# One PSUM buffer of two banks for the side work of the second state pass

## The chip, the cores and the metric

The kernel runs on one core of a Trainium2 chip. The metric is device time in microseconds (us) from launch to end. The median of three runs of the kernel before is 1549.19 us.

## What is computed

The reference works in three steps on x (8 batches, 8 heads, 512 tokens, 64 dimensions) and on a state of 32 rows per batch and head.

```python
scores = scale * x @ state.T          # each token reads the 32 states
xread  = softmax(scores) @ state
sread  = softmax(scale * state @ x.T) @ x   # each state reads the 512 tokens
x = concat([xread, sread])            # 8 * 544 rows of 512
x = (sigmoid(x @ w_gate) * (x @ w_val)) @ w_out      # 512 -> 1536 -> 512
out = relu(x @ w_in) ** 2 @ w_out2                   # 512 -> 2048 -> 512
```

Products are made from two fp32r parts of each operand (a high part and the rest), three matmuls for one product.

## The kernel before, in words

**Rewriting.** The rows xread are never multiplied by the gate and value weights. As xread is softmax times state, the kernel multiplies the state by the weights first (state_weights, L466) and the 512 softmax rows of a batch by the small result (front_x, L550). The gate and value weights come in 6 chunks `ch` of 256 columns, each in 4 row pieces `c` (a pair of heads), so a pass over them is 24 pieces. The states of batches 0 to 3 are the first half (m = 0), those of batches 4 to 7 the second (m = 1). There are two passes over the weights, one for each half. The change concerns the second.

**A piece of the second pass.** chunk_steps (L496) lists the steps of a chunk: load 256 KB of gate and of value weights (L118), convert them into a high and a low part (`w`, L149 on ScalarE and L150 on VectorE), then state_weights and store_g. state_weights (L466) takes two PSUM tiles `ps[0]` and `ps[1]`, called ps_g in the profile, and issues six matmuls at L474, for i in three products and in each for j in two halves: half j uses rows 64j to 64j+63 of the state and the weights and writes `ps[j]`. For i = 0 and 2 the weights' high part is read, for i = 1 the low part. Then ScalarE copies `ps[0]` (L478) and, when m is 1, VectorE copies `ps[1]` (L480) into `go`. store_g (L485) writes `go` to a DRAM tile gd; load_g (L529) reads it back as `gi`, and split_gw (L535) makes `gg` of it, the operand of front_x.

**PSUM.** The eight banks are divided among three pools: `acc` has four, `mm` two, and `at` two buffers of one bank. Every piece of work beside the units takes its tiles from `at`: state_weights (ps_g), the transposes of the states (ps_st, L231), of x (ps_xt, L306, batches 0 to 2 alone), the scores (a3, L322, ps_s2, shown as ps_s in the profile), the transposes of the other softmax (b5, L379, ps_e), the state reads (b6, L404, ps_sr) and their transposes (b7, L426, ps_so).

**Order.** The main stream of the gated layer is 108 units `(b, f)`: front (gate and value matmuls psg and psv, sigmoid, product, split) and back1 (the output matmuls into acc). Units 0 to 47 serve batches 0 to 3 and 48 to 95 batches 4 to 7; the last twelve serve the state rows. A unit calls step() six times, and step() runs what is due in `queue`, which spread() fills: a list of functions evenly over a stretch given in units. In units 25 to 55 run the six chunks of the second pass, five units for each. The scores work att_a of batch 4 is spread over units 33 to 40, of 5 over 40 to 47, of 6 over 47 to 54, of 7 over 54 to 61. The state reads att_b of batch 0 are spread over units 48 to 53.4, and each further batch starts five units later; by unit 96, split_states (L569) needs all of them. The results of the second pass are needed from unit 48 (chunk 0) to unit 58 (chunk 5, batch 4).

This list is the order of the source. The order in which each engine runs its instructions is settled when the program is built, by the framework's scheduler (`schedule_with_timeline_sim=True` in the launch): it moves an instruction ahead of others whose operands or buffers it doesn't expect to be ready. On the chip, each engine keeps to that order.

Of the kernel before, what the change touches and what calls it, by code (L numbers as in the profile page):

```python
# [8 lines left out]
F32 = mybir.dt.float32  # L9
# [6 lines left out]
PSUM = bass.MemoryType.PSUM  # L16
DRAM = bass.MemoryType.DRAM

P = 128
# [14 lines left out]
def kernel(  # L34
# [22 lines left out]
    B, H, S, D = x.shape  # L57
# [26 lines left out]
    dram = ctx.enter_context(tc.tile_pool(name="dram", bufs=1, space=DRAM))  # L84
    acc_p = ctx.enter_context(tc.tile_pool(name="acc", bufs=1, space=PSUM))
    mm_p = ctx.enter_context(tc.tile_pool(name="mm", bufs=2, space=PSUM))
    at_p = ctx.enter_context(tc.tile_pool(name="at", bufs=2, space=PSUM))


    one = ctx.enter_context(ExitStack())  # L90
# [20 lines left out]
    def load_raw(src):  # L111
        raw = raw_p.tile([P, 512, 2], U32, tag="raw", name="raw")
        flat = raw.rearrange("p a b -> p (a b)")
        for cols, ap in src:
            to = flat[:, cols]
            if len(ap.shape) == 3:
                to = to.rearrange("p (k f) -> p k f", k=ap.shape[1])
            nc.sync.dma_start(out=to, in_=ap)  # L118
        return raw
# [34 lines left out]
    def row_src(w, f):  # L154
        return [(every, w.bitcast(U32)[f * P : (f + 1) * P, :])]
# [35 lines left out]
    def mm3(ps, lh, ll, rh, rl, start, stop):  # L191
        nc.tensor.matmul(ps, lh, rh, start=start, stop=False)  # L192
        nc.tensor.matmul(ps, lh, rl, start=False, stop=False)  # L193
        nc.tensor.matmul(ps, ll, rh, start=False, stop=stop)  # L194
# [33 lines left out]
        return raw  # L228

    def prep_states(m, raw):  # L230
        ps = at_p.tile([P, 512], F32, tag="at", name="ps_st")  # L231
        for c in range(NPAIR):
            cs = slice(c * P, (c + 1) * P)
            nc.tensor.transpose(ps[:, cs], raw[:, cs], ident)
        h, l = (st_t[:, i, m].rearrange("p c n -> p (c n)") for i in range(2))
        nc.scalar.copy(out=h, in_=ps)
        nc.vector.tensor_sub(out=l, in0=ps, in1=h.bitcast(F32))
# [51 lines left out]
    def group_stages(b, g):  # L289
# [13 lines left out]
        def a2(p):  # L303
            def run():
                if by_pe:
                    xf = at_p.tile([P, S], F32, tag="at", name="ps_xt")  # L306
                    for t in range(NT):
                        ts = slice(t * P, (t + 1) * P)
                        nc.tensor.transpose(xf[:, ts], loaded_x[b, g][:, p, t, :], ident)
                else:  # L310
                    xf = f_p.tile([P, S], F32, tag="xf", name="xf", bufs=1)
                    nc.vector.transpose(xf, loaded_x[b, g][:, p, :])
                h = xx_p.tile([P, S], F32R, tag="xth", name="xth")
                l = xx_p.tile([P, S], F32R, tag="xtl", name="xtl")
                nc.scalar.copy(out=h, in_=xf)
                nc.vector.tensor_sub(out=l, in0=xf, in1=h.bitcast(F32))
                v["xt", p] = (h, l)

            return run

        def a3():
            ps = at_p.tile([P, 512], F32, tag="at", name="ps_s2")  # L322
            for p in range(2):
                h, l = v.pop(("xt", p))
                d = diag[:, :, 2 * g + p, :]
                mm3(ps, d[:, 0], d[:, 1], h, l, p == 0, p == 1)
            s2 = f_p.tile([P, S], F32, tag="s2", name="s2", bufs=1)
            nc.scalar.copy(out=s2, in_=ps)
            v["s2"] = s2
# [46 lines left out]

        def b5():
            e2 = v.pop("e2")
            ps = at_p.tile([P, 512], F32, tag="at", name="ps_e2")  # L379
            for t in range(NT):  # L380
                ts = slice(t * P, (t + 1) * P)
                nc.tensor.transpose(ps[:, ts], e2[:, ts], ident)
            et = f_p.tile([P, NT, 2, 2, 64], F32R, tag="et", name="et", bufs=1)
            pv = ps.rearrange("p (t c n) -> p t c n", t=NT, c=2)
            nc.scalar.copy(out=et[:, :, :, 0, :], in_=pv)
            nc.vector.tensor_sub(
                out=et[:, :, :, 1, :], in0=pv, in1=et[:, :, :, 0, :].bitcast(F32)
            )
            v["et"] = et
# [11 lines left out]
        def b6(p):  # L401
            def run():
                et, xs = v["et"], v.pop(("xs", p))
                ps = at_p.tile([P, 512], F32, tag="at", name="ps_sr")  # L404
                pv = ps[:, : 4 * D]
                for t in range(NT):
                    nc.tensor.matmul(
                        pv,
                        et[:, t, p].rearrange("p l n -> p (l n)"),
                        xs[:, :, :, t, :],  # L410
                        start=(t == 0),
                        stop=(t == NT - 1),
                    )
                tmp = f_p.tile([64, 2, P], F32, tag="tmp", name="tmp", bufs=1)
                if p == 0:
                    v["w"] = f_p.tile([64, 2, P], F32, tag="sw", name="sw", bufs=1)
                sv = pv.rearrange("p (l m) -> p l m", l=2)
                nc.scalar.copy(out=tmp, in_=sv[64:128])
                nc.vector.tensor_add(out=tmp, in0=sv[:64], in1=tmp)
                nc.vector.tensor_add(out=v["w"][:, p], in0=tmp[:, 0, :], in1=tmp[:, 1, :])  # L420

            return run

        def b7():
            w = v.pop("w")
            ps = at_p.tile([P, 2, 64], F32, tag="at", name="ps_so")  # L426
            for p in range(2):
                nc.tensor.transpose(ps[:, p, :], w[:, p, :], ident[:64, :64])
            for p in range(2):
                for i in range(2):  # L430
                    to = xs_t[D * p : D * (p + 1), 2 * g + i, b * NS : (b + 1) * NS]
                    src = ps[D * i : D * (i + 1), p, NS * i : NS * (i + 1)]
                    if i:
                        nc.scalar.copy(out=to, in_=src)
                    else:
                        nc.vector.tensor_copy(to, src)
# [29 lines left out]
    def state_weights(ch, c, m):  # L466
        w = gv.pop((ch, c))
        if m:
            nc.sync.dma_start(out=w_dram[ch, c], in_=w.bitcast(F32))
        ps = [at_p.tile([P, 512], F32, tag="at", name="ps_g") for j in range(2)]  # L470
        for i, (l, r) in enumerate(((0, 0), (0, 1), (1, 0))):
            for j in range(2):
                rows = slice(D * j, D * (j + 1))
                nc.tensor.matmul(  # L474
                    ps[j], st_t[rows, l, m, c, :], w[rows, r, :], start=(i == 0), stop=(i == 2)
                )
        o = go_p.tile([P, 2, 512], F32, tag="go", name="go")
        nc.scalar.copy(out=o[:, 0, :], in_=ps[0])  # L478
        if m:
            nc.vector.tensor_copy(o[:, 1, :], ps[1])  # L480
        else:
            nc.scalar.copy(out=o[:, 1, :], in_=ps[1])
        g_out[ch, c, m] = o
# [12 lines left out]
    def chunk_steps(ch, m, outs):  # L496

        raws = {}  # L500
        jobs = [("p", c) for c in range(NPAIR)] + [("o", f) for f in outs]
        steps = []

        def load(n):
            k, i = jobs[n]
            raws[n] = load_raw(pair_src(ch, i) if k == "p" else row_src(w_out1, i))

        def conv(n):
            k, i = jobs[n]
            if k == "p":  # L510
                conv_gv(ch, i, raws.pop(n))
            else:
                conv_out1(i, raws.pop(n))

        steps += [lambda: load(0), lambda: load(1)]
        for n in range(len(jobs) + 2):
            if n < len(jobs):
                steps.append(lambda n=n: conv(n))
                if n + 2 < len(jobs):
                    steps.append(lambda n=n: load(n + 2))  # L520
            if 1 <= n <= NPAIR:
                steps.append(lambda n=n: state_weights(ch, n - 1, m))
            if 2 <= n <= NPAIR + 1:
                steps.append(lambda n=n: store_g(ch, n - 2, m))
        return steps
# [244 lines left out]
    def spread(fns, start, end):  # L770

        for i, fn in enumerate(fns):
            queue.append((STEPS * (start + (end - start) * i / max(len(fns), 1)), len(queue), fn))
# [39 lines left out]
    second = []  # L813
    spread([lambda: second.append(load_states(1))], 21.5, 21.5)
    spread([lambda: prep_states(1, second.pop())], 23.5, 23.5)
    for ch in range(NCH):
        spread(chunk_steps(ch, 1, []), 25 + 5 * ch, 30 + 5 * ch)
    for b in range(QB, B):
        start = 33 + 7 * (b - QB)
        spread(att_a[b], start, start + 7)  # L820
# [96 lines left out]
```

## Time and profile before

| | |
|---|---|
| median of 3 runs | 1549.19 us (1548.54 to 1552.41) |
| the profiled execution | 1554.75 us, span 1553.0 us |
| mean granted TensorE clock | 0.980 |
| TensorE (PE) busy | 1502.7 us, 97% of the span |
| VectorE (DVE) busy | 856.6 us, 55% |
| ScalarE (ACT) busy | 724.5 us, 47% |
| second pass, first to last ps_g matmul | 246.7 to 492.9 us |

Times are us from the start of the span. PE stands for matmuls, PEld for their weight loads, SP for the DMA queue. Matmuls of a stream overlap: a row's own length (some 0.39 us) is longer than the distance from one start to the next (0.23 us), so costs on PE are taken from starts. The releaser that a row names is what ended the idle time of its engine.

### The profile page before, as it was taken

The numbers are of one execution on the slowest core, as the hardware profiler recorded it, in microseconds if no ns is written. First come the engines' busy times: TensorE is split into PE (matmuls) and PEld (weight loads), VectorE is DVE, ScalarE is ACT, GpSimd is POOL, SyncE is SP. The second block draws the span as 40 slices with busy tenths as digits, with TensorE's granted clock in tenths as the row PEclk, the third lists the DMA queues.
The fourth block names the chain that finished last, engine by engine and source line by source line (L and its number), as shares of the span: only waits on it lengthen the run. The fifth ranks groups of instructions, "written<-read, shape, count | busy, mean of one in ns | idle before, by whom it ended". The sixth has DMA issues, their size and how long they took to land.

```text
span 1553.0 us, 19161 instructions
## 1 busy us (share of the span) xinstructions
PE 1502.7 (97%) x6760; PEld 1198.6 (77%) x6760; DVE 856.6 (55%) x1550; ACT 724.5 (47%) x1314; POOL 215.2 (14%) x263
## 2 busy tenths in 40 slices
PE   5889999999998999999999999999999999999998
PEld 3568766777776778888898788888888888888887
DVE  7986896778986655555649832323232323323232
ACT  5676765456676877665435522223232222223222
POOL 1123223212332343343000000000000000000000
PEclk9789999999998999999999999999999999999999
DMA  9783788879976433342925300101010000101000
GB/s 275 232 223 96 214 275 266 275 241 256 283 209 163 147 89 111 82 122 70 392 94 159 121 27 1 55 0 54 1 55 0 28 28 0 55 0 41 1 28 15
DMA packets 173106, 185.82 MB, mean 120 GB/s; under 512 B 99537, under 2 KB 108753, under 8 KB 171985
## 3 DMA queue, kind: packets, MB, share of 16 engines
q1 hardware_dynamic: 170928, 184.07, 38.9%
q8 instruction: 53, 0.87, 0.2%
q10 hardware_dynamic: 2080, 0.52, 0.2%
q14 instruction: 45, 0.36, 0.1%
HBM read 120.59 MB, written 63.96 MB: 119 GB/s over the span
## 4 chain that ended last, share of the span: by engine, by line
PE 86%; DVE 5%; DMA 4%; ACT 2%; issue 1%; SPq 1%; POOL 0%; DVEq 0%; ACTq 0%
PE acc L193 13%; PE acc L192 13%; PE acc L194 13%; PE psi L194 8%; PE psi L192 8%; PE psi L193 8%; PE psv L192 3%; PE psg L192 3%; PE ps_g L474 3%; PE psv L193 3%; PE psv L194 3%; PE psg L193 3%; PE psg L194 3%; DMA raw<-in_moe_w_val_dram 2%; DMA gd<-go 1%
## 5 line engine op out<-in xcount | busy, mean ns | idle before, releaser
L200 DVE TENSOR_TENSOR gl<-g,gh 128x512 fp32r<-128x512 f32 (+1 forms) x252 | 181.1, 719 | 233.6 <-ACT gh L199 220.9
L199 ACT CAST gh<-g 128x512 fp32r<-128x512 f32 (+1 forms) x252 | 150.3, 596 | 241.8 <-PE acc L193 212.6
L725 DVE TENSOR_TENSOR g<-r 128x512 f32<-128x512 f32 (+1 forms) x144 | 95.4, 662 | 233.9 <-ACT r L724 233.8
L192 PE MATMUL psi<-xh,wi 128*128 128x512 f32 (+1 forms) x576 | 217.7, 378 | 2.1 <-ACT wi L149 2.1
L194 PE MATMUL psi<-xh,wi 128*128 128x512 f32 (+1 forms) x576 | 217.3, 377 | 0.2 <-DVE wi L150 0.2
L193 PE MATMUL psi<-xl,wi 128*128 128x512 f32 (+1 forms) x576 | 217.3, 377 | 0.0
L541 POOL TENSOR_TENSOR gg<-gi,gg 128x256 fp32r<-128x256 f32 x192 | 157.6, 840 | 399.6 <-ACT gg L540 392.1
L192 PE MATMUL acc<-wu,gh 128*128 128x512 f32 x544 | 212.1, 390 | 0.8 <-ACT gh L199 0.8
L193 PE MATMUL acc<-wu,gh 128*128 128x512 f32 x544 | 211.9, 389 | 0.0
L724 ACT ACTIVATE r<-psi 128x512 f32<-128x512 f32 (+1 forms) x144 | 82.7, 574 | 275.0 <-PE psi L194 275.0
L194 PE MATMUL acc<-wu,gl 128*128 128x512 f32 x544 | 206.3, 389 | 0.0
L193 PE MATMUL acc<-gl,o 128*128 128x512 f32 (+1 forms) x432 | 164.9, 383 | 1.9 <-DVE gl L200 1.8
L194 PE MATMUL acc<-gh,o 128*128 128x512 f32 (+1 forms) x432 | 163.1, 379 | 0.0
L192 PE MATMUL acc<-gh,o 128*128 128x512 f32 (+1 forms) x432 | 143.2, 386 | 0.7 <-ACT gh L199 0.7
L192 PEld LDWEIGHTS psi<-xh,wi 128*128 128x128 f32 x576 | 108.3, 188 | 24.1 <-ACT wi L149 3.8
L194 PEld LDWEIGHTS psi<-xh,wi 128*128 128x128 f32 x576 | 108.5, 188 | 20.7 <-DVE wi L150 0.7
L193 PEld LDWEIGHTS psi<-xl,wi 128*128 128x128 f32 x576 | 108.3, 188 | 20.4
L192 PEld LDWEIGHTS acc<-wu,gh 128*128 128x128 f32 x544 | 102.2, 188 | 22.5 <-ACT gh L199 1.7
L194 PEld LDWEIGHTS acc<-wu,gl 128*128 128x128 f32 x544 | 102.0, 188 | 21.3
L193 PEld LDWEIGHTS acc<-wu,gh 128*128 128x128 f32 x544 | 102.3, 188 | 20.5
L193 PEld LDWEIGHTS acc<-gl,o 128*128 128x128 f32 x432 | 81.3, 188 | 21.8 <-DVE gl L200 3.5
L192 PEld LDWEIGHTS acc<-gh,o 128*128 128x128 f32 x432 | 80.5, 190 | 20.3 <-issue 2.4
(122 smaller groups left out, 2433.1 us busy)
## 6 DMA issues: line engine op xcount, KB each, us to landing
gd<-go SPq DMA_DIRECT2D x192, 128.0 KB, 3.5
gi<-gd SPq DMA_DIRECT2D x96, 256.0 KB, 3.7
raw<-in_moe_w_out_dram SPq DMA_DIRECT2D x28, 512.0 KB, 4.6
raw<-in_moe_w_gate_dram SPq DMA_DIRECT2D x48, 256.0 KB, 4.4
raw<-in_moe_w_val_dram SPq DMA_DIRECT2D x48, 256.0 KB, 4.5
wd<-w SPq DMA_DIRECT2D x24, 512.0 KB, 4.3
ws<-wd SPq DMA_DIRECT2D x24, 512.0 KB, 8.7
xn<-in_x_dram SPq DMA_DIRECT2D x32, 256.0 KB, 3.7
```

The lines of the kernel that those rows point to most:

```text
L192: nc.tensor.matmul(ps, lh, rh, start=start, stop=False)
L193: nc.tensor.matmul(ps, lh, rl, start=False, stop=False)
L194: nc.tensor.matmul(ps, ll, rh, start=False, stop=stop)
L199: nc.scalar.copy(out=gh[:, :n], in_=g32[:, :n])
L200: nc.vector.tensor_sub(out=gl[:, :n], in0=g32[:, :n], in1=gh[:, :n].bitcast(F32))
L474: nc.tensor.matmul(ps[j], st_t[rows, l, m, c, :], w[rows, r, :], start=(i == 0), stop=(i == 2))
L541: nc.gpsimd.tensor_sub(out=t[:, 1, g], in0=src, in1=t[:, 0, g].bitcast(F32))
L724: nc.scalar.activation(out=r[:, :n], in_=ps[:, :n], func=AF.Relu)
L725: nc.vector.tensor_mul(out=g32[:, :n], in0=r[:, :n], in1=r[:, :n])
```

## The change

The pool `at` becomes a pool that is closed and opened again. From unit 24.5 to 25 on (open_at(True)) it has one buffer of two banks; from unit 55.1 on (open_at(False)) it has two buffers of one bank again. While it has the one, state_weights takes a single tile of two banks, and `ps[0]` and `ps[1]` are its halves; every other user (at_tile) takes such a tile too and uses its first bank. The matmuls, copies and DMAs are the same in kind and number, and so is the source order. In six more places (a2, a3, b5, b6, b7, prep_states) only the allocation is replaced by at_tile.

```diff
--- before.py
+++ after.py
@@ -84,7 +84,28 @@
     dram = ctx.enter_context(tc.tile_pool(name="dram", bufs=1, space=DRAM))
     acc_p = ctx.enter_context(tc.tile_pool(name="acc", bufs=1, space=PSUM))
     mm_p = ctx.enter_context(tc.tile_pool(name="mm", bufs=2, space=PSUM))
-    at_p = ctx.enter_context(tc.tile_pool(name="at", bufs=2, space=PSUM))
+
+    at = {}
+
+    def open_at(both):
+        if at:
+            at["pool"].close()
+        at["pool"], at["both"] = ExitStack(), both
+        at["tiles"] = at["pool"].enter_context(
+            tc.tile_pool(name="at", bufs=1 if both else 2, space=PSUM, reuse_waits="tile")
+        )
+
+    open_at(False)
+    ctx.callback(lambda: at["pool"].close())
+
+    def at_tile(name, shape=(P, 512)):
+        if at["both"]:
+            flat = at["tiles"].tile([P, 2, 512], F32, tag="at", name=name)[:, 0, :]
+        else:
+            flat = at["tiles"].tile([P, 512], F32, tag="at", name=name)
+        if len(shape) == 3:
+            flat = flat[:, : shape[1] * shape[2]].rearrange("p (a b) -> p a b", a=shape[1])
+        return flat
 
 
     one = ctx.enter_context(ExitStack())
@@ -228,7 +249,7 @@
         return raw
 
     def prep_states(m, raw):
-        ps = at_p.tile([P, 512], F32, tag="at", name="ps_st")
+        ps = at_tile("ps_st")
         for c in range(NPAIR):
             cs = slice(c * P, (c + 1) * P)
             nc.tensor.transpose(ps[:, cs], raw[:, cs], ident)
...
@@ -467,7 +488,11 @@
         w = gv.pop((ch, c))
         if m:
             nc.sync.dma_start(out=w_dram[ch, c], in_=w.bitcast(F32))
-        ps = [at_p.tile([P, 512], F32, tag="at", name="ps_g") for j in range(2)]
+        if at["both"]:
+            both = at["tiles"].tile([P, 2, 512], F32, tag="at", name="ps_g")
+            ps = [both[:, j, :] for j in range(2)]
+        else:
+            ps = [at_tile("ps_g") for j in range(2)]
         for i, (l, r) in enumerate(((0, 0), (0, 1), (1, 0))):
             for j in range(2):
                 rows = slice(D * j, D * (j + 1))
@@ -813,8 +838,10 @@
     second = []
     spread([lambda: second.append(load_states(1))], 21.5, 21.5)
     spread([lambda: prep_states(1, second.pop())], 23.5, 23.5)
+    spread([lambda: open_at(True)], 24.5, 25)
     for ch in range(NCH):
         spread(chunk_steps(ch, 1, []), 25 + 5 * ch, 30 + 5 * ch)
+    spread([lambda: open_at(False)], 55.1, 56)
     for b in range(QB, B):
         start = 33 + 7 * (b - QB)
         spread(att_a[b], start, start + 7)
```

## Rows read from the trace of the kernel before

**Rows 1.** The page: busy us, share of the span, instructions.

```profile
PE 1502.7 (97%) x6760; PEld 1198.6 (77%) x6760; DVE 856.6 (55%) x1550; ACT 724.5 (47%) x1314; POOL 215.2 (14%) x263
```

**Rows 2.** Stretches: us, busy by engine (instructions), granted clock, DMA share, GB/s.

```profile
300.00:400.00 100.00, 100.00 (x405) 71.44 (x404) 81.82 (x140) 59.88 (x106) 25.21 (x32) 1.00 0.86 267
400.00:430.00 30.00, 30.00 (x122) 20.99 (x121) 26.66 (x49) 19.56 (x34) 8.65 (x12) 1.00 0.90 256
...
490.00:500.00 10.00, 5.91 (x24) 4.07 (x22) 3.66 (x8) 3.88 (x7) 1.26 (x1) 0.74 0.76 203
500.00:510.00 10.00, 9.85 (x36) 7.76 (x37) 5.95 (x11) 8.49 (x18) 6.01 (x7) 0.75 0.46 106
```

**Rows 3.** The chain that ended last, from 246 to 494 us, by line.

```profile
by line: PE ps_g L474 15.7%; PE acc L193 13.3%; PE acc L192 13.1%; PE acc L194 12.8%; PE psg L192 7.3%; PE psv L192 7.3%; PE psg L194 6.5%; PE psg L193 6.4%; PE psv L193 6.2%; PE psv L194 6.1%; DMA gd<-go 1.2%; PE ps_s L193 1.2%; PE ps_s L1
```

**Rows 4.** Tile ps_g, 246 to 494 us: duration ns min/median/max, first and last start.

```profile
L474 PE MATMUL ps_g<-w,st_t x144: 386/394/502, 246.7 to 492.5; 64*128 64x512 f32 x144
```

**Rows 5.** PE's timeline: start us, us, what; a piece whose six matmuls stand together.

```profile
275.28 0.39 PE L194 MATMUL psg<-a,gg 128*128 128x512 f32 x1
275.60 0.97 PE L474 MATMUL ps_g<-w,st_t 64*128 64x512 f32 x6
...
276.82 0.39 PE L193 MATMUL psg<-a,gg 128*128 128x512 f32 x1
```

**Rows 6.** PE's timeline: halves of pieces, three matmuls at a time.

```profile
338.18 0.39 PE L192 MATMUL psg<-a,gg 128*128 128x512 f32 x1
338.50 0.96 PE L474 MATMUL ps_g<-w,st_t 64*128 64x512 f32 x3
...
339.73 0.39 PE L194 MATMUL psg<-a,gg 128*128 128x512 f32 x1
...
342.12 0.96 PE L474 MATMUL ps_g<-w,st_t 64*128 64x512 f32 x3
```

**Rows 7.** PE's timeline: four matmuls (two of each half), and two (one of each).

```profile
263.07 0.39 PE L194 MATMUL psg<-a,gg 128*128 128x512 f32 x1
263.39 0.74 PE L474 MATMUL ps_g<-w,st_t 64*128 64x512 f32 x4
...
264.40 0.40 PE L193 MATMUL psv<-a,gg 128*128 128x512 f32 x1
...
368.45 0.40 PE L194 MATMUL acc<-gh,o 128*128 128x512 f32 x1
368.77 0.50 PE L474 MATMUL ps_g<-w,st_t 64*128 64x512 f32 x2
...
369.55 0.40 PE L193 MATMUL psg<-a,gg 128*128 128x512 f32 x1
```

**Rows 8.** PE's timeline: first and last use of `at` in the crowded stretch, three holders.

```profile
316.37 0.39 PE L192 MATMUL ps_s<-xth,diag 128*128 128x512 f32 x1
...
430.85 0.60 PE L382 MATMUL ps_e<-ident,e 128*128 128x128 f32 x4
...
450.30 0.27 PE L428 MATMUL ps_so<-ident,sw 64*128 64x64 f32 x1
...
491.92 0.96 PE L474 MATMUL ps_g<-w,st_t 64*128 64x512 f32 x3
```

**Rows 9.** ScalarE's timeline: the copies that end two of these holds.

```profile
323.37 0.59 ACT L328 COPY s<-ps_s 128x512 f32<-128x512 f32 x1 [1.53 <-PE ps_s L194]
...
457.94 0.18 ACT L434 COPY xs_t<-ps_so 64x32 f32<-64x32 f32 x1
```

**Rows 10.** PE's timeline: idle time before an instruction and its releaser, 494 to 745 us.

```profile
494.87 1.22 PE L407 MATMUL ps_sr<-xs,et 128*128 128x256 f32 x4 [1.40 <-DVE et L386]
498.41 1.22 PE L407 MATMUL ps_sr<-xs,et 128*128 128x256 f32 x4 [2.32 <-POOL xs L396]
500.15 0.79 PE L192 MATMUL psg<-a,gg 128*128 128x512 f32 x1 [0.52 <-ACT gg L540]
...
744.64 0.39 PE L192 MATMUL psg<-sp,ws 128*128 128x256 f32 x1 [1.06 <-ACT sp L571]
```

More of the change, by code (lines that the diff above doesn't have):

```diff
@@ L305, in run @@
                 if by_pe:
-                    xf = at_p.tile([P, S], F32, tag="at", name="ps_xt")
+                    xf = at_tile("ps_xt")
                     for t in range(NT):
@@ L321, in a3 @@
         def a3():
-            ps = at_p.tile([P, 512], F32, tag="at", name="ps_s2")
+            ps = at_tile("ps_s2")
             for p in range(2):
@@ L378, in b5 @@
             e2 = v.pop("e2")
-            ps = at_p.tile([P, 512], F32, tag="at", name="ps_e2")
+            ps = at_tile("ps_e2")
             for t in range(NT):
@@ L403, in run @@
                 et, xs = v["et"], v.pop(("xs", p))
-                ps = at_p.tile([P, 512], F32, tag="at", name="ps_sr")
+                ps = at_tile("ps_sr")
                 pv = ps[:, : 4 * D]
@@ L425, in b7 @@
             w = v.pop("w")
-            ps = at_p.tile([P, 2, 64], F32, tag="at", name="ps_so")
+            ps = at_tile("ps_so", (P, 2, 64))
             for p in range(2):
```

## Prediction

> **What bounds the kernel.** I read the page first: PE is busy for 97% of the span, no other engine above 55% [rows 1]. That is a mean, so I asked for the stretch in which the second pass runs, some 246 to 494 us. From 300 to 430 us PE has no idle time at the full clock, VectorE is busy for 82 and then 89% and the DMA engines for 86 and 90% [rows 2]. The stage is bound by PE, with VectorE and the transfers 10 to 18% behind. Then the chain that ended last: its largest entry there, 15.7%, is the state_weights matmul of L474 [rows 3], ahead of any line of the main units, though it has only 144 matmuls there, six for each of 24 pieces [rows 4]. They cost more than their number. The timeline of PE says why, and I followed it through.
>
> A piece whose six matmuls stand together starts them in pairs: half 0 and half 1 use different rows of the array and run side by side. From the matmul before it to the second one behind it is 276.82 - 275.28 = 1.54 us [rows 5]. Two steps of the plain stream are 2 x 0.23 = 0.46 (0.455), so the visit costs **1.09 us**. Where three matmuls of one half stand alone, the same distance is 339.73 - 338.18 = 1.55, so also 1.09, for half the work; the next three stand 342.12 - 338.50 = 3.6 us later at the same price [rows 6]. Two pairs cost 264.40 - 263.07 - 0.455 = 0.87, one pair 369.55 - 368.45 - 0.455 = 0.65 [rows 7]. The price of a visit goes by how many starts follow one another, and a pair is one start.
>
> Counting all visits from 246.7 to 491.9 us in that timeline, I find 50 for the 24 pieces: 33 at about 1.08, seven at 0.86, nine at 0.63 and one at 1.31, together 48.7 us, or 2.03 a piece. Only three pieces stand whole in one visit. The first 20 pieces (42 visits, to 430 us) cost 40.3, the last four (8 visits) 8.4.
>
> **What the change does.** It adds and removes no matmul, copy or transfer.
>
> *The two halves get their PSUM at the same moment.* Before, each half takes a buffer of its own, and a half whose buffer is still to be emptied is placed later. With one tile of two banks a piece has both or neither. Six matmuls in a row cost 1.09: 24 x 1.09 = 26.2, a saving of 22.5 us. That is the upper end. The halves share the weights' state, though: matmuls 3 and 4 need the low part, which comes after the high one, so a piece with its buffer ready early may go as two matmuls and then four: 0.65 + 0.87 = 1.52, or 36.5 in all, a saving of 12.2. That is the lower end. I take 18 whole and 6 split pieces, since most halves stand by threes now, high and low together, so the weights are there and the buffer is late: 18 x 1.09 + 6 x 1.52 = 28.7, a saving of **20.0**: 16.4 in the first 20 pieces (40.3 - 20 x 1.195) and 3.6 in the last four.
>
> Of the 16.4 I count all, since PE does not idle there and what is next is behind it by more: it is some 9% of PE's time from 246.7 to 430 us, and VectorE and DMA are 10 to 18% below. If VectorE took over in the worst part, 400 to 430 us, PE could still give back 30.0 - 26.7 = 3.3 us there [rows 2], and its 9% are 2.7.
>
> *One user of `at` at a time.* Until unit 48 the buffer is shared with four a3 only. One a3 holds a bank from 316.37 to 323.96 (its copy's 323.37 + 0.59) [rows 8, 9], 7.6 us, and a piece that meets it now waits whole, where it used one bank for both halves in turn. Behind a visit that the built order puts ahead of an empty buffer, PE and all main matmuls behind it wait. A piece comes every 10 us ((492.5 - 246.7) / 24 [rows 4]), so a delay of 7.6 us is made good before the next; I cost it at nothing until 431 us, and at 7.6 us once if it falls on a piece that is late for its store.
>
> From unit 48 on the state reads join. From the first ps_e at 430.85 to the last half piece at 491.92 + 0.96 = 492.9, 14 users take `at` in 62 us [rows 8]: two ps_e, four ps_sr, two ps_s, two ps_so and four pieces. That is 4.4 us for each, with two buffers. One ps_so alone holds its bank from 450.30 to 458.12, 7.8 us [rows 8, 9]: four small copies that alternate between two engines. Bounds for this stretch with one buffer: if one such hold that lies beside other users today moves into the line, it becomes 7.6 us longer; if instead each piece takes its turn once where its halves take two, it becomes four visits shorter, 4 x 1.09 = 4.4. I take 2 us later, near the middle, as the users already stand behind one another most of the time.
>
> *What waits for it.* The last piece is stored, read back, split, and only then has unit 58 its operand. Before, that is a stall already: PE waits 1.40, 2.32 and 0.52 us [rows 10], in 490 to 510 us it is busy for 5.9 and 9.9 of 20, and the granted clock, a mean of the levels 1.2 and 2.4 GHz, falls to 0.74 and 0.75 there, after the idle time [rows 2]. The store and the read-back stand in SP's queue with the weight loads, so they gain nothing by an earlier PE. So behind 431 us the chain through `at` sets the end, not PE: the last four pieces' 3.6 us turn into waiting, and the 2 us are lost in full. The same holds at unit 96, where PE waits for split_states, which waits for the last state read (1.06 us [rows 10]): no slack there, no new gain either.
>
> *Opening and closing the pool* issues nothing; the first tile of the new pool waits for the last of the old. At unit 55 this is one more place in the same line of users, in the 2 us.
>
> Sum on the profiled execution: 1554.75 - 16.4 + 2 = 1540.4. The median of the runs is 5.56 below that execution (1549.19), so **1535 us**.
>
> The Trainium skill (Perfetto Trace Analysis, Matmuls under Optimizing Tensor Performance) says that independent matmul groups should rotate through different PSUM banks, so that one is emptied while the next is computed. That speaks against a single buffer; by it the fourth case below is the likeliest, at 1556. Here PE has the units' matmuls in `mm` and `acc` to run while `at` is emptied, and shows no idle time in 300 to 430 us [rows 2], so I give it a small chance.
>
> **The cases.** A measurement of this kernel can tell about 0.3%, 4.6 us, from no change.
>
> 1. *The forecast*, 0.56: 1535, from 1530 (all whole: 2.1 more for the first 20, 3 from the chain) to 1541 (all split: 40.3 - 30.4 = 9.9, less 2).
> 2. *All of it*, 0.16: whole pieces and a chain through `at` that becomes shorter, since a piece holds it once. Then 22.5 us go in full, 1527. For it: two halves that wait in turn for one bank. Against it: the users that are now alone in a line.
> 3. *The saving is not passed on or not made*, 0.16: VectorE or the transfers (89 and 90% at 400 us [rows 2]) take over, or the halves stand apart for another reason than their banks, the order being settled at build. PE then idles, or still makes some 40 visits. A gain of 2 to 4 us: 1546.
> 4. *The line before the one buffer is longer*, 0.12: slower. Six a3 at up to 7.6 us and two ps_so at 7.8 [rows 8, 9] each hold up a piece whole; 6 x 7.6 + 2 x 7.8 = 61 us of holds. If the half of them that may lie beside other users today moved into the line, the last piece would leave some 30 us later than now after equal PE work; PE saves 20 to 23 by then, so some 7 us more than all the saving turn into a stall: 1556. It decides from where that delay passes 20 us.
>
> Range: 1526 to 1551 takes in the first three cases with their bounds; what is outside is the fourth and the far end of the second. Faster by over 0.3% are the first two, 0.72; the third is the same, 0.16; slower is the fourth, 0.12. The likeliest case's own range is 1530 to 1541.
>
> **What would show it.** In the second pass, L474 stands in 24 to 30 visits, most of six matmuls, and unit 48 begins some 16 us earlier. If visits stay near 50, the third case holds. If they fall and unit 48 is not earlier, PE waits on VectorE or a transfer, and the idle time names which. The gap ahead of psg by unit 58 is the test of the second part: about 2 to 6 us more idle by the forecast, 15 or more in the fourth case, less than now in the second. After 560 us nothing should change but the start; if the wait before split_states grows beyond a few us, the state reads were set back. The forecast is wrong if the total is above 1544 or below 1527.

## The result and the profile after

The changed kernel takes **1559.18 us** (median of four runs, 1558.38 to 1562.28) where the kernel before takes 1550.80 beside it: 1.0063 times as long, with a 95% interval of [1.0049, 1.0076]. The forecast was 1535, the range 1526 to 1551. It became slower, by the fourth case, which had 1556 and a chance of 0.12.

The profiled executions stand at 1554.75 us before and 1559.75 after, spans 1553.0 and 1558.0. The 5.0 us between them are what the readings below have to explain; the medians are some 8 apart, as the profiled execution of before was longer than the four that the median is of.

The page answers to [rows 1]: the work on PE became 17.6 us less, and the span longer.

```profile
PE 1485.1 (95%) x6760; PEld 1190.4 (76%) x6760; DVE 854.9 (55%) x1550; ACT 720.9 (46%) x1314; POOL 216.5 (14%) x263
```

Stretches of the changed kernel, with the columns of [rows 2]:

```profile
300.00:400.00 100.00, 96.73 (x424) 72.77 (x424) 84.46 (x144) 59.78 (x108) 28.45 (x36) 1.00 0.87 264
400.00:430.00 30.00, 28.71 (x133) 21.60 (x132) 25.00 (x45) 17.28 (x34) 6.93 (x9) 1.00 0.85 259
430.00:470.00 40.00, 35.03 (x157) 27.49 (x156) 25.20 (x47) 25.25 (x45) 10.55 (x12) 1.00 0.44 113
470.00:490.00 20.00, 11.53 (x50) 7.66 (x50) 15.41 (x29) 10.66 (x18) 4.60 (x6) 0.78 0.70 209
490.00:500.00 10.00, 6.56 (x22) 3.58 (x18) 6.04 (x10) 4.22 (x8) 1.62 (x2) 0.50 0.59 109
500.00:515.00 15.00, 9.49 (x36) 7.35 (x37) 6.25 (x17) 8.41 (x19) 5.81 (x6) 0.72 0.59 157
515.00:700.00 185.00, 182.87 (x852) 148.95 (x852) 109.54 (x207) 133.49 (x253) 71.91 (x79) 1.00 0.38 111
```

The same stretches of the kernel before, from 430 us:

```profile
430.00:470.00 40.00, 40.00 (x179) 31.17 (x179) 34.27 (x63) 30.38 (x57) 13.57 (x14) 1.00 0.81 214
470.00:490.00 20.00, 20.00 (x84) 14.48 (x83) 16.64 (x28) 11.87 (x21) 6.69 (x9) 1.00 0.43 119
490.00:500.00 10.00, 5.91 (x24) 4.07 (x22) 3.66 (x8) 3.88 (x7) 1.26 (x1) 0.74 0.76 203
500.00:515.00 15.00, 14.85 (x60) 11.96 (x61) 8.19 (x17) 12.96 (x25) 7.33 (x8) 0.83 0.42 105
```

Read down the second column. From 430 to 515 us PE is busy for 80.8 of 85 us before and for 62.6 after: 18 us of idle time that is new, with the granted clock at 0.78, 0.50 and 0.72 in it. The transfers are set back with it: their share is 0.44 instead of 0.81 from 430 to 470 us, and 0.70 instead of 0.43 from 470 to 490.

**The pairing did what was forecast.** The timeline of PE has a whole piece at the old price; it answers to [rows 5]:

```profile
278.73 0.39 PE L215 MATMUL psg<-a,gg 128*128 128x512 f32 x1
279.05 0.97 PE L499 MATMUL ps_g<-w,st_t 64*128 64x512 f32 x6
...
280.28 0.40 PE L214 MATMUL psv<-a,gg 128*128 128x512 f32 x1
```

280.28 - 278.73 - 0.455 = 1.09. Counted as before, 28 visits stand for the 24 pieces, 21 of them of six matmuls; the first 20 pieces cost 24.9 us (forecast 23.9, before 40.3). From the first psg matmul of each unit, unit 48 begins at 401.6 instead of 414.1 and unit 57 at 465.4 instead of 479.5: PE is **14.1 us ahead** (1.2 of them already at unit 24, ahead of the pairs). Unit 57 then lasts 26.6 us instead of 7.1, unit 58 18.9 instead of 17.6, and unit 59 begins at 510.9 instead of 504.3: **6.6 behind**. At unit 96 it is 5.0 behind (749.6 instead of 744.6), and so is the end. All was gained by unit 57 and lost, with more, in two units; 19.5 us of it in unit 57, behind which PE waits for the first half of unit 58's operand.

The timeline of PE shows what stands before that. From 387 to 400 us:

```profile
387.27 0.47 PE L213 MATMUL ps_s<-xth,diag 128*128 128x512 f32 x1 [0.24 <-DVE go L505]
...
394.42 0.39 PE L215 MATMUL ps_s<-xth,diag 128*128 128x512 f32 x1
...
399.72 0.96 PE L499 MATMUL ps_g<-w,st_t 64*128 64x512 f32 x6
```

The a3 of batch 5 takes the one buffer at 387.27 and gives it back when ScalarE has copied it, at 397.23:

```profile
396.65 0.58 ACT L349 COPY s<-ps_s 128x512 f32<-128x512 f32 x1
```

That is a hold of 10.0 us, from the first write to the end of the copy that empties the buffer. Chunk 3's last piece was at 378.35 us, where its halves were at 388.7 and 394 before, so the side work, that is all users of `at`, was 10 us ahead. Chunk 4's first piece is at 399.72, where its first half was at 399.77 before: behind this a3, that lead is gone.

The a3 is not the only long holder. The piece ahead of it is written at 378.35 and emptied by VectorE's copy of its second half:

```profile
386.44 0.68 DVE L505 COPY go<-ps_g 128x512 f32<-128x512 f32 x1
```

That is 8.8 us, and the a3 begins right behind it. The other pieces from 372 to 430 us hold the buffer for 5.0 to 7.5 us each, counted in the same way. From 372.70 to 446.32 it stands empty for 8.5 of 73.6 us. Then the line of the state reads, which is what I call the users of `at` from the first ps_e to chunk 5's last piece:

```profile
429.65 0.66 PE L403 MATMUL ps_e<-ident,e 128*128 128x128 f32 x4 [0.93 <-DVE go L505]
...
436.52 0.64 PE L428 MATMUL ps_sr<-xs,et 128*128 128x256 f32 x4
...
446.32 0.39 PE L213 MATMUL ps_s<-xth,diag 128*128 128x512 f32 x1
...
471.08 0.96 PE L499 MATMUL ps_g<-w,st_t 64*128 64x512 f32 x6
...
477.68 0.96 PE L499 MATMUL ps_g<-w,st_t 64*128 64x512 f32 x6 [0.91 <-DVE tmp L440]
...
489.29 1.65 PE L499 MATMUL ps_g<-w,st_t 64*128 64x512 f32 x6 [1.30 <-ACT xs_t L455]
...
494.86 1.65 PE L499 MATMUL ps_g<-w,st_t 64*128 64x512 f32 x6
...
505.55 0.80 PE L213 MATMUL psg<-a,gg 128*128 128x512 f32 x1 [3.90 <-ACT gg L565]
```

It begins 1.2 us earlier than before (430.85 [rows 8]) and ends at 496.5 instead of 492.9: 66.9 us instead of 62. The second half of unit 58's operand comes 5.40 us later than in [rows 10]. Three of the four pieces stand right behind a user of another kind, and two rows name it: the state reads' `tmp`, and the last copy of a ps_so. The second piece, which completes the first half of that operand, is at 477.68, where its last half was at 466.39 before. The first ps_sr is the longest hold of this line. It starts at 436.52 and is emptied only at 445.60, by VectorE's second reading of it, which waits for ScalarE's copy; and that copy stands in ScalarE's order behind an exp that waited for a DMA:

```profile
440.74 1.28 ACT L389 ACT_TABLE_LOAD   x1 [1.14 <-DMA e<-sd]
442.03 0.72 ACT L389 ACTIVATE e<-e,nm 128x512 f32<-128x512 f32 x1
...
444.78 0.37 ACT L439 COPY tmp<-ps_sr 64x256 f32<-64x256 f32 x1
```

```profile
445.18 0.42 DVE L440 TENSOR_TENSOR tmp<-ps_sr,tmp 64x256 f32<-64x256 f32 x1 [1.95 <-ACT tmp L439]
```

### The profile page after: what moved, and what is told of

Its sections match the earlier page's. It is cut to its first block, busy times and chain, and to the rows that moved or that the text cites. A ratio compares the mean times of both kernels' runs of the same rounds, so it can differ in the third digit from the quotient of the medians.

```text
span 1558.0 us, 19134 instructions
## 1 busy us (share of the span) xinstructions
PE 1485.1 (95%) x6760; PEld 1190.4 (76%) x6760; DVE 854.9 (55%) x1550; ACT 720.9 (46%) x1314; POOL 216.5 (14%) x263
## 4 chain that ended last, share of the span: by engine, by line
PE 72%; DVE 12%; DMA 8%; ACT 3%; issue 3%; SPq 1%; POOL 1%; DVEq 0%; ACTq 0%; POOLq 0%
PE acc L214 11%; PE acc L213 11%; PE acc L215 11%; PE psi L215 8%; PE psi L213 8%; PE psi L214 8%; PE psg L213 2%; PE psg L214 2%; PE psv L213 2%; PE psv L214 2%; PE psg L215 2%; PE psv L215 2%; DMA raw<-in_moe_w_val_dram 2%; DMA raw<-in_moe_w_out_dram 1%; DMA gd<-go 1%
## 5 line engine op out<-in xcount | busy, mean ns | idle before, releaser
L215 PE MATMUL acc<-gh,o 128*128 128x512 f32 (+1 forms) x432 | 163.1, 379 | 0.0
L213 PE MATMUL acc<-gh,o 128*128 128x512 f32 (+1 forms) x432 | 136.7, 382 | 3.9 <-ACT gh L220 3.6
L149 ACT ACTIVATE q<-raw 128x512 uint16<-128x512 uint32 x92 | 73.1, 794 | 51.0 <-DVE c L167 26.4
```

The lines of the kernel that those rows point to most:

```text
L149: nc.scalar.activation(out=q[:, :, 0], in_=lo, func=AF.Copy, scale=2.0**-29)
```

## The experiments

Each edit is against the changed kernel unless it says otherwise. Ratios are to the kernel before, timed on the same chip; those of the medians alone differ from them by up to 0.13%, inside the intervals.

**Where the loss sits: the stretch with one buffer.** Four kernels change only the stretch.

*To unit 49.3, so that the state reads have two buffers:*

```diff
-    spread([lambda: open_at(False)], 55.1, 56)
+    spread([lambda: open_at(False)], 49.3, 49.4)
```

> The one buffer of two banks ends at unit 49.3 of the source order, after the last piece of chunk 4 and before the first ps_e; chunk 5 and the state reads have two buffers again. Theory A (the state reads in one line with the last four pieces give the gain back): the saving of the first 20 pieces stays, PE reaches unit 48 some 12 us earlier than before and the stall by unit 58 is as before, so about 1538 us against 1550.8 of the kernel before. Theory B (VectorE or the transfers hold the pieces back, so that PE's saving is not passed on): 1549 to 1551. Theory C (the cost is a3 in the one buffer): about 1545, and less good than the next run.

Measured: 1552.06 us, 1.0008 [0.9997, 1.0020]. The loss is gone, but no gain appears, so the state reads in one line are not all of it. (It is about the time that theory B gives, by which PE's saving is not passed on; the next run speaks against that.) The a3 of batch 5 still holds the buffer from 390.37, and the first ps_e is where it was before:

```profile
390.37 0.47 PE L213 MATMUL ps_s<-xth,diag 128*128 128x512 f32 x1 [0.24 <-DVE go L505]
...
402.81 0.96 PE L499 MATMUL ps_g<-w,st_t 64*128 64x512 f32 x6
...
431.22 0.60 PE L403 MATMUL ps_e<-ident,e 128*128 128x128 f32 x4
```

*To unit 45.3, ahead of that a3 too:*

```diff
-    spread([lambda: open_at(False)], 55.1, 56)
+    spread([lambda: open_at(False)], 45.3, 45.4)
```

> The one buffer ends at unit 45.3, after the last piece of chunk 3 and before the a3 of unit 45.8. Theory A: the saving of 16 pieces instead of 20, about 10 us: 1541. Theory B: 1549 to 1551. Theory C: better than the run until 49.3, about 1538.

Measured: **1543.16 us, 0.9946 [0.9930, 0.9961]**, the best of all: it beats both kernels. Chunk 4's pieces stand in halves again, the first of them between the matmuls of the a3, which the single buffer forbids:

```profile
387.43 0.40 PE L213 MATMUL ps_s<-xth,diag 128*128 128x512 f32 x1
387.76 0.96 PE L499 MATMUL ps_g<-w,st_t 64*128 64x512 f32 x3
...
394.01 0.39 PE L215 MATMUL ps_s<-xth,diag 128*128 128x512 f32 x1
395.46 0.96 PE L499 MATMUL ps_g<-w,st_t 64*128 64x512 f32 x3
...
420.05 0.66 PE L403 MATMUL ps_e<-ident,e 128*128 128x128 f32 x4
```

The first ps_e comes 10.8 us earlier than before, the last half piece ends 9.3 earlier (483.6), unit 59 begins 8.9 earlier (495.4), and the total is 7.7 to 8.4 less. It pays the price of some 1.09 for each half of the last eight pieces, and is still faster: from the a3 on, a lead of the side work is worth more than a lead of PE.

*Only from 49.3 to 55.1, so that the state reads alone pay:*

```diff
-    spread([lambda: open_at(True)], 24.5, 25)
+    spread([lambda: open_at(True)], 49.3, 49.4)
```

> The one buffer only from unit 49.3 to 55.1: the cost of the crowded stretch without the gain ahead of it. Theory A: slower than the changed kernel, by the 12 us or so that it no longer gains ahead of it, 1566 to 1572; the stall by unit 58 is over 25 us. Theories B and C: no slower than the changed kernel, 1555 to 1560, since there is little ahead of it to lose and only one a3 in it.

Measured: 1562.92 us, 1.0065 [1.0048, 1.0081]. One buffer among the state reads costs some 10 us by itself (12 by the medians), less than theory A had and more than the others. By the ratios the whole kernel, with 15 us saved in its first 20 pieces, is as slow as this one.

*To unit 62.1, so that the line goes on:*

```diff
-    spread([lambda: open_at(False)], 55.1, 56)
+    spread([lambda: open_at(False)], 62.1, 63)
```

> The one buffer lasts to unit 62.1 instead of 55.1, so the state reads of batch 1 and part of batch 2 and the a3 of batch 7 go through it as well, while no piece is left to pair. Theory A, if the state reads themselves are paced by the buffer: each batch of state reads takes longer, the wait at split_states grows, 1565 to 1580. If only the pieces behind the state reads count (the operand of unit 58), the same as the changed kernel within 3 us, 1559.

Measured: 1577.93 us, 1.0168 [1.0146, 1.0189]. Now the state reads come too late for unit 96 as well. The timeline of PE has the waits; the stretch from 740 to 770 us has it busy for 9.43 of 30 (the columns of [rows 2]):

```profile
755.77 1.22 PE L428 MATMUL ps_sr<-xs,et 128*128 128x256 f32 x4 [6.00 <-POOL xs L417]
...
765.92 0.58 PE L213 MATMUL psg<-sp,ws 128*128 128x256 f32 x1 [3.04 <-ACT sp L596]
```

```profile
740.00:770.00 30.00, 9.43 (x40) 7.22 (x39) 16.23 (x37) 13.69 (x28) 3.85 (x3) 0.59 0.58 200
```

**The a3's share: moved out of the way.** The scores of batches 5 to 7 are put 9.4 units later, with the buffer's stretch to 49.3 (first edit) and then to 55.1 as in the changed kernel (second edit alone):

```diff
-    spread([lambda: open_at(False)], 55.1, 56)
+    spread([lambda: open_at(False)], 49.3, 49.4)
...
-        start = 33 + 7 * (b - QB)
+        start = 33 + 7 * (b - QB) + (9.4 if b > QB else 0)
```

> The one buffer until unit 49.3, and the scores work of batches 5 to 7 is 9.4 units later in the source order, so that in the stretch of the one buffer only the two a3 of batch 4 remain. Theory C (what kept the run until 49.3 from gaining is the a3 of batch 5 that holds the one buffer, with the four pieces of chunk 4 waiting): these pieces and the first ps_e come some 10 us earlier, at about 420 us for the ps_e, and the time is 1541 to 1545. Rival (the whole two-bank pieces of chunk 4 are themselves slower than halves, with a copy on VectorE that comes late): the ps_e stays at 429 to 431 and the time at 1550 to 1554.

> The changed kernel (one buffer until 55.1) with the same move of the scores work. Theory A (the state reads ahead of the last four pieces in one line cost about 10 us whatever a3 does): 8 to 12 us slower than the run e9, the last piece 55 to 65 us behind the first ps_e. Rival (a3 is the whole cost of the one buffer): within 3 us of e9.

Measured: 1547.01 us, 0.9981 [0.9968, 0.9993], and 1553.34, 1.0024 [1.0013, 1.0035]. By the ratios the first is 4 us and the second 6 us better than its like with the a3 in place (1.0008 and 1.0063). In the first, chunk 4's pieces follow one another every 6.6 to 6.9 us and stand whole (each holds the buffer for 6.1 to 6.4 us of that, so its own hold is now nearly the whole distance), and the state reads begin 21 us earlier than in the kernel with the a3 in place:

```profile
390.02 0.96 PE L499 MATMUL ps_g<-w,st_t 64*128 64x512 f32 x6
...
396.91 0.97 PE L499 MATMUL ps_g<-w,st_t 64*128 64x512 f32 x6
...
403.53 0.97 PE L499 MATMUL ps_g<-w,st_t 64*128 64x512 f32 x6
...
410.00 0.60 PE L403 MATMUL ps_e<-ident,e 128*128 128x128 f32 x4
```

The direction is that of the theory, the total is not the 21 us: unit 59 begins 15.4 us earlier (486.0 instead of 501.4), but unit 96 only 2.9 (737.6 instead of 740.5), and its wait for split_states grew from 1.05 to 3.05 us. In the second the line of the state reads still takes 71.3 us (407.41 to 478.71), with one a3 in it instead of two, and the kernel is 6.3 us slower than the first: that is again the price of one buffer among the state reads. The edit moves all the scores work of three batches, with its conversions and copies, and it was not tried with two buffers throughout; how much of the 4 and 6 us the move is worth without the a3's hold stays open.

**Can the holds be made shorter?** *The a3 in the other order,* second half of its operand first, as 3.0 us lie between its two halves in the changed kernel (starts at 389.56 and 392.60), in which PE does a unit's matmuls:

```diff
-            for p in range(2):
+            for p in (1, 0):
...
-                mm3(ps, d[:, 0], d[:, 1], h, l, p == 0, p == 1)
+                mm3(ps, d[:, 0], d[:, 1], h, l, p == 1, p == 0)
```

with the stretch to 49.3, and, as a control, the same in the kernel before.

> The kernel with the one buffer until unit 49.3, and a3 does the pair p = 1 first, whose operand is made last, so that all its matmuls stand together and its tile is held for about 2 us instead of 4 to 10. Theory C1 (what kept the run until 49.3 from gaining is the hold of a3 at unit 45.8, 390.4 to 399.7 us, with the pieces of chunk 4 behind it): those pieces come 5 to 8 us earlier and the time falls from 1552 to 1543 to 1546. Theory C2 (chunk 4 is late because its two-bank tiles wait for the later of two copies, whatever a3 does): within 3 us of 1552.

> Control: the same edit of a3 in the kernel before, with two buffers of one bank throughout. Both theories: within 3 us of 1550.8, since a piece finds the other bank while a3 holds one.

Measured: 1555.54 us, 1.0038 [1.0023, 1.0052], and 1560.61, 1.0070 [1.0055, 1.0085]. The hold became shorter, 6.4 us instead of 9.3, but it began later and ended later (402.34 instead of 399.66), so nothing could be gained. The control was to be within 3 us and became 11 us slower. PE doesn't idle from 200 to 430 us in it, and yet it is 2.8 us behind the kernel before at unit 48; it is 5.5 behind at unit 57, 9.9 at unit 59 and 5.4 at unit 96. From 430 to 515 us PE idles 9.2 us, where it idles 4.2 before:

```profile
430.00:470.00 40.00, 37.40 (x162) 27.79 (x161) 28.96 (x58) 28.64 (x50) 9.73 (x10) 1.00 0.70 193
470.00:515.00 45.00, 38.41 (x150) 27.10 (x149) 29.84 (x54) 26.51 (x50) 12.71 (x16) 0.85 0.66 170
```

So the pair tells nothing about holds. It tells that an edit which only exchanges two halves, with two buffers throughout, moves this kernel by 11 us; the order of all engines is settled anew. Why this order is worse was not looked into.

*The copy of ps_sr on VectorE,* so that it doesn't stand behind ScalarE's exp:

```diff
-                nc.scalar.copy(out=tmp, in_=sv[64:128])
+                nc.vector.tensor_copy(tmp, sv[64:128])
```

> The changed kernel, with the first copy out of ps_sr made by VectorE instead of ScalarE, where it stood 7.6 us behind an exponential that waits for a transfer (ps_sr at 436.5, its copy at 444.8 us). Theory D1 (the line of users is long because the copies that free the buffer stand in ScalarE's fixed order): the line from the first ps_e to the last piece shrinks from 66 us to 55 to 60, and the time falls by 4 to 9 us to 1550 to 1555. Theory D2 (the line is set by the state reads' own steps, conversions and transfers, not by the copies): within 3 us of 1559.

Measured: 1562.76 us, 1.0084 [1.0069, 1.0100]. The first ps_sr holds the buffer for 5.6 us instead of 9.1 (435.16 to 440.72), and the line stays at 67.6 us (428.50 to 496.1). That hold was not what made the line long: behind it the buffer now stands empty for 3.8 us ahead of the a3 at 444.49 and for 4.2 ahead of the ps_sr at 451.51, users that wait for their own operands.

**Can the reads be moved?** Each batch 3.5 units later, so that chunk 5's pieces go first:

```diff
-        start = 48 + 5 * b
+        start = 51.5 + 5 * b
```

> The changed kernel with the state reads 3.5 units later in the source order (51.5 + 5b instead of 48 + 5b), so that most pieces of chunk 5 stand ahead of them in the line. Theory A: the last piece comes 25 to 35 us earlier, the stall by unit 58 goes (unit 59 starts at about 485 instead of 511), and since the state reads need 36 us a batch whatever PE does and are due at unit 96, part comes back there as a wait of 10 to 15 us: about 1546. Rival (unit 58 waits for the transfers and conversions of chunk 5 and not for the buffer): the last piece moves less than 8 us, and the time is 1559 or more.

Measured: 1560.40 us, 1.0069 [1.0048, 1.0090]. The last piece is at 477.93, 16.9 us earlier, unit 59 begins 17.5 earlier (493.4), and all of it is lost at unit 96, where PE waits for the state reads and is busy for 49.74 of 70 us:

```profile
700.00:770.00 70.00, 49.74 (x271) 42.46 (x270) 41.68 (x93) 36.21 (x70) 10.86 (x10) 0.83 0.59 202
```

**Can the best be bettered?** *The pairs from unit 12 on,* to unit 45.3, so that the last pieces of the first pass stand whole too:

```diff
-    spread([lambda: open_at(True)], 24.5, 25)
+    spread([lambda: open_at(True)], 12.05, 12.1)
...
-    spread([lambda: open_at(False)], 55.1, 56)
+    spread([lambda: open_at(False)], 45.3, 45.4)
```

> The one buffer from unit 12.1, in the first pass over the weights as well, to unit 45.3. In the first pass 12 pieces stand in 18 visits from 155 to 235 us, 1.09 us each, and no state reads and no a3 share the buffer. Theory A (pairing is worth its visits wherever PE is the bound and no other user shares the buffer): 5 to 6 us faster than the run until 45.3, 1537 to 1539. Rival: the first pass is bound by the transfers or by both copies on ScalarE there, then 1542 to 1545.

Measured: 1551.50 us, 1.0012 [1.0003, 1.0021]. Unit 24 begins at 230.0 us instead of 236.5, but unit 44 at 374.5 instead of 369.8. The same stretch, first of this kernel, then of the one with pairs from 24.5 to 45.3 only:

```profile
240.00:300.00 60.00, 56.06 (x245) 41.25 (x245) 44.71 (x80) 29.70 (x60) 17.65 (x21) 0.97 0.88 290
```

```profile
240.00:300.00 60.00, 60.00 (x267) 44.26 (x266) 45.14 (x77) 29.89 (x59) 18.33 (x23) 1.00 0.88 292
```

With the transfers at 0.88 and some 290 GB/s in both, PE now idles in one and not in the other: here a faster PE does meet another limit. Its two longest waits there, 1.18 us at 255.67 and 2.08 at 268.73, are for ScalarE, which ahead of the first had itself waited 5.53 us for the read-back `gi`. The one buffer is a rival: from 215.29 to 241.47 four pieces hold it for 5.5 to 7.0 us each, with 0.05 us between them. Which of the two sets the pace was not separated.

*The pieces faster,* a chunk in 4.6 units instead of 5, the stretch to 43.0:

```diff
-        spread(chunk_steps(ch, 1, []), 25 + 5 * ch, 30 + 5 * ch)
-    spread([lambda: open_at(False)], 55.1, 56)
+        spread(chunk_steps(ch, 1, []), 25 + 4.6 * ch, 29.6 + 4.6 * ch)
+    spread([lambda: open_at(False)], 43.0, 43.1)
```

> A version that may beat both: the run e2, with the six chunks of the second pass 4.6 units long instead of 5, so that the last pieces come 2.4 units earlier in the source order, and the one buffer until unit 43.0, again behind chunk 3. If the buffer's users set when the last piece comes: most of the stall that is left by unit 58 (19.1 us for a unit of 7) goes, 1534 to 1539. If the transfers (0.87 to 0.93 of the DMA engines' time in that run) hold the pieces back: within 3 us of 1543, with more idle time of PE before 430 us.

Measured: 1545.46 us, 0.9969 [0.9956, 0.9983]. The last ps_g matmul starts at 466.0 us and the stall at unit 58 is gone (PE idles 3.7 us from 430 to 515 instead of 5.8), but PE idles 6.8 us from 700 to 770 us instead, 3.13 of them in the wait for split_states at 737.32. From 300 to 430 us it idles 4.7 us instead of 3.0, which is the sign named for pieces held back by the transfers. No better than the stretch to 45.3 alone.

## Why the prediction was wrong

**The two halves at the same moment: right.** 21 whole pieces and 28 visits; 15.4 us saved in the first 20 pieces where 16.4 were forecast.

**That VectorE and DMA are behind PE by more: right in 300 to 400 us,** where PE idles for 3.3 us in all and unit 57 starts 14.1 us earlier. The kernel with pairs from unit 12 shows how near a limit was: from 240 to 300 us it idles 3.9 us, the changed one 0.3.

**"A piece comes every 10 us ..., so a delay of 7.6 us is made good before the next; I cost it at nothing until 431 us": this step failed first.** The hold was 10 us, longer than the 7.6 of [rows 8, 9] (the same a3 held its bank for 8.4 us before, 399.45 to 407.87), and as long as the mean distance between pieces. That mean was no measure of the gaps: in the changed kernel the pieces of a chunk come closer, at 372.70 and 378.35 for example, and with one tile each holds the buffer for 5.0 to 8.8 us itself, a hold that the sum does not have at all. The a3 also stood where it was needed to be out of the way: behind chunk 3 and ahead of the line of the state reads. A delay of PE is made good by idle time; a delay of the side work is made good only if its line has gaps, and this line had 8.5 us of them in 73.6, up to 446 us. By their ratios, two pairs of kernels put the a3's share at 4 us (1.0008 against 0.9981) and 6 us (1.0063 against 1.0024), a third, with the stretch cut to 45.3, at 10 (1.0008 against 0.9946). None of them is that hold alone: the first two move the whole scores work, and the third gives chunk 4's pieces two buffers as well.

**"Behind 431 us the chain through `at` sets the end, not PE": right, and not used.** I let the line begin 16.4 us earlier, as PE did, and added 2. But if the chain through `at` is the limit behind 431 us, its start must come from the same chain: it began 1.2 us earlier. From that alone, with the line's 62 us unchanged, the forecast would have had a gain of 1.2 us.

**The line of the state reads, +2 us between -4.4 and +7.6: mis-sized.** It took 66.9 us, +4.8, inside the bounds. By their ratios the kernels put the price of one buffer there, on the whole time, at 10 us (1.0065 for that stretch alone), 8.5 us (1.0063 against 1.0008) and 7 us (1.0024 against 0.9981). That is more than 4.8. The length of the line was the wrong term for it: unit 58 needs the second piece first, and that stands 11.3 us later than before (477.68 against 466.39), the last one 3.6 later. The sum also left out that the waiting PE also runs at a lower clock: 0.50 from 490 to 500 us, where [rows 2] have 0.74. How much of the loss is the clock and how much the waits was not separated.

**The case that came: the fourth,** "the line before the one buffer is longer": 1556, 3 us from the result, by the place named (the gap ahead of psg by unit 58 and what leads to it). The size is partly luck: it had the last piece 30 us later after equal PE work against 20 to 23 us saved, the trace has 17.7 (14.1 and 3.6) against 14.1 ahead, and its holders were the a3 and the ps_so, not the pieces. Its chance was argued away with one sentence, that PE shows no idle time in 300 to 430 us because the units' matmuls cover it. That is true of PE and does not touch the line. The rule of the Trainium skill that stood beside it (Perfetto Trace Analysis, Matmuls under Optimizing Tensor Performance: rotate independent groups through different banks) is borne out by the runs: two buffers in place of one among the state reads are worth 7 to 10 us, and the pieces of [rows 6], in halves, are dearer on PE and yet the better choice there.

**The test of the gap** was put as 2 to 6 us more idle by the forecast and 15 or more in the fourth case. PE idles 18 us more from 430 to 515 us, but spread over two units; ahead of the psg matmul itself the row has 3.90. A gap that is shared out over many short waits must be read from a stretch, not from one row.

**Behind 560 us nothing changed but the start: right.** The wait before split_states is 1.05 us, beside 1.06 in [rows 10].

What is shown: the saving on PE, its loss in units 57 and 58, and that a stretch which ends before the shared use keeps a gain, 0.54% in one build and 0.31% in another (the pieces faster). What stays open is how the loss divides: each re-built order carries its own effect, up to 11 us in the control, so a share of 5 us from a single pair of kernels could be chance. Three pairs for the a3 (4 to 10 us) and three for the state reads (7 to 10 us) agree in sign and roughly in size, and the shares rest on that and on the holds in the traces; the gain of 0.54% is measured, but some of it may be such an effect too.

## What to carry to other kernels

Before buffers are merged for one user, list all users of the pool in order, the one that the merge is for among them, with the hold of each from its first write to the end of the copy that empties it, and ask whether that line has gaps; where it has few, a hold that grows delays all behind it. A saving on the busiest engine is worth something only up to the next operand that comes by another line: work out when that line starts from its own users. And a scheme that is good in one stretch can be limited to it: the same pairs, given up ten units earlier, turned 0.63% of loss into 0.54% of gain.

## What the runs showed of the hardware

Three matmuls of one half alone cost PE 1.09 us [rows 6], as much as the six of a whole piece, 1.09 before the change [rows 5] and after it. Where PE waited for the side work in 470 to 515 us, in many short waits of 0.8 to 3.9 us, the granted clock fell to 0.50 in the worst stretch, all of it at the lower level of 1.2 GHz, and it was 1.00 again from 515 us on. A buffer's hold is set less by the matmuls than by the copies behind them: the first ps_sr is written in 0.64 us and held for 9.1, because its copy's turn on ScalarE came behind another wait; with the copy on VectorE it was 5.6. I had taken holds from two rows of the crowded stretch, 7.6 and 7.8 us; the runs had 10.0 for the a3, 9.1 for the first ps_sr and 5.0 to 8.8 for the pieces from 372 to 430 us, which I had not counted.
